# Phase-2 loads kept in program order, and 96-row reads of the normalised activations into alternating partition ranges

## The chip, the cores and the metric

One Trainium2 chip, one core of it. The metric is the device time of one execution in microseconds (us); lower is better. Engines: PE (TensorE matmul, with PEld its weight loads), ACT (ScalarE), DVE (VectorE), POOL (GpSimd), SP (SyncE, which here only issues DMAs). Each engine works through its own queue in order.

## The reference

```
out = depthwise 3x3 convolution of x          # x: 1 x 512 x 512 x 96, bf16
h   = layernorm(out)                          # over the 96 channels
h   = gelu(h @ w1)                            # 96 -> 384
gx  = sqrt(sum over all pixels of h*h + 1e-6) # one number per hidden channel
nx  = gx / (mean of gx + 1e-6)
h   = gamma * (h * nx) + beta + h
out = x + h @ w2                              # 384 -> 96
```

`nx` needs a sum over the whole image, so nothing of the last product can begin before the GELU of every pixel has been squared and summed.

## The kernel before

The image is cut into 128 blocks of 4 rows (2048 pixels), and the kernel runs in two phases.

**Phase 1** goes through the blocks in slots, as a software pipeline. In each slot there are steps of several blocks: load x, transpose it (DVE), convolve (PE), copy out of PSUM (ACT), square (POOL or ACT), statistics (PE), normalise (`stage_norm`, POOL). `stage_write` (SP, four DMAs of 96 KB) stores the normalised block to DRAM as `yn_dram[q]`, 96 channels by 2048 pixels; `stage_read` (SP, one DMA of 384 KB) brings it back into one of six ring tiles `yn_ring` (profile name `ynT`), channels on partitions 0-95. Then comes the MLP step: `w1` times the block (PE), GELU (ACT), the sums of squares (DVE `bn_stats`, or PE products of the result with itself, "gram"). The last 14 blocks use `mlp_tail`: four PE/ACT units per block. Step order for a block b: normalise in slot s, write in s+1, read in s+2, MLP in s+4; in each slot SP gets the reads before the writes. So at the end SP's program order is: read of 125, write of 126, read of 126, write of 127, read of 127, then five loads of x (`xr`) for phase 2 and the first phase-2 load of `ynT`.

**Between the phases** DVE reduces the sums (`second_moments`, `junk` for the gram diagonal, a Newton root), scales `w2` into `W2s`, and phase 2's products can start. Ahead of that, POOL has made the first three `xb` tiles (x plus bias; three buffers).

**Phase 2** makes the output blocks in the order `ORDER` = 123, 125, 127, 118, 1, 2, 0, 4, 5, 120, 6, 8, 3, ... Of 128 blocks, 35 have their GELU output stored in DRAM (`g_dram`, loaded as `gl`, 1536 KB, issued by POOL), 5 are still in SBUF, and 88 are computed again (`recompute`, `cm_unit`: per quarter block three matmuls of 512 columns with `ynT` and `w1p`, and one GELU `gr`). Three of the 88 (123, 125, 127) still have their ring tile; the other 85 read it again (`load_rest`, line 294, SP). That read takes 128 rows, the 96 of the block and 32 of the next one, and rows 96-127 of `w1p` are zero. For position n of `ORDER` the loop at lines 1007-1019 issues the loads of position n+5 (`load_rest`, `load_xr` by POOL), makes `xb` of position n+2 (`stage_xb`, POOL), does 48 small matmuls per block (`stage_mm2`, PE) with four DVE additions into `o_sb`, and stores `o_sb` (`stage_out`, SP). Units of the recomputation are dealt out between the matmuls (`pace`, at least 6 ahead of the even pace).

**What sets the order.** The instructions are placed on each queue by a scheduler that simulates the program and prefers the earlier traced instruction among those ready. Engines wrapped in `InOrder` (`pe, dve, act, pool, sp`) pin each instruction behind the one traced before it on its engine. Phase 1 uses only the wrapped engines. The phase-2 loop uses the wrapped PE, DVE and ACT, but the bare `nc.sync` and `nc.gpsimd` for loads, `xb` and stores, so these may be placed anywhere that their data and buffers allow, ahead of phase-1 instructions too. In the profile wrapped instructions have the line of the wrapper, L35; bare ones keep theirs (L294 `ynT`, L290 `gl`, L279 `xr`, L324 `xb`, L352 stores).

DMAs that SP and ACT issue take eight completion semaphores in turn; a DMA whose semaphore is still in use by the eighth transfer before it carries a wait for that one.

**Setup.** ACT issues the loads of `w1` (three DMAs of 32 rows into `w1_raw`), `w2`, gamma and beta, ahead of its first copy of a convolution. `setup_mlp` (slot 3) subtracts the column mean from `w1` with one DVE instruction and writes `w1p`. `setup_ynt` clears partitions 96-127 of the ring tiles (POOL).

Of the kernel before, what the change touches and what calls it, by code (L numbers as in the profile page):

```python
# [8 lines left out]
ALU = mybir.AluOpType  # L9
# [3 lines left out]
GR = 4  # L13
# [43 lines left out]
def kernel(  # L57
# [10 lines left out]
    nc = tc.nc  # L68
# [53 lines left out]
    def yn_src(q):  # L122
        return yn_dram[q].rearrange("c (r w) -> c r w", r=GR)

    def yn_rows(q):
        return yn_dram[q:q + 2].rearrange("q c (r w) -> (q c) r w", r=GR)[0:128]

    def yn_dst(q, r):
        return yn_dram[q].rearrange("(c i) (r w) -> r c i w", i=NI, r=GR)[r]

# [5 lines left out]
    dwx = consts.tile([9, NI, GR, 32], bf16, name="dwx")  # L136
    eye32 = consts.tile([128, 32], bf16, name="eye32")
    rowsel = consts.tile([128, GR], bf16, name="rowsel")
    w1_raw = consts.tile([C, E], bf16, name="w1_raw")
    w1p = consts.tile([128, E], bf16, name="w1p")  # L140
    Wq = consts.tile([128, NI, 3, GR, 32], bf16, name="Wq")
    w2_sb = consts.tile([128, NCH, C], bf16, name="w2_sb")
    gam_bf = consts.tile([128, NCH], bf16, name="gam_bf")
# [40 lines left out]
    with ExitStack() as p1:  # L184
# [98 lines left out]
        def load_rest(n, sq, pq):  # L283
            q = ORDER[n]
            v = grp.setdefault(q, {})
            if is_held(q):
                v["g"] = gs[q]
            elif is_whole(q):
                v["g"] = late.gl.tile([128, NQ, NCH, QW], bf16, name="gl")
                pq.dma_start(out=v["g"][:].rearrange("p t j w -> p (t j w)"), in_=g_dram[whole.index(q)])  # L290
            else:
                ynt = yn_ring[SLOTS[nth_made[q] % NYT]]
                if q not in KEPT:
                    sq.dma_start(out=ynt[:], in_=yn_rows(q))  # L294
                v["ynt"] = ynt

        def recompute(q, t):
            if t == 0:
                grp[q]["g"] = late.gr.tile([128, NQ, NCH, QW], bf16, name="gr")
            cm_unit(grp[q]["g"], grp[q]["ynt"], t)  # L300

        def cm_unit(g, ynt, t):
            U = banks3()
            for j in range(NCH):
                pe.matmul(quad_out(U[:, j, :]), lhsT=w1p[:, j * 128:(j + 1) * 128],
                          rhs=quad(ynt[:], t), start=True, stop=True)
            act.activation(out=g[:, t, :, :], in_=U, func=ACTF.Gelu_apprx_tanh)

        def px_unit(g, ynt, t):
            Uf = banks3().rearrange("p k w -> p (k w)")  # L310
            for r in range(GR):
                c = r * E
                while c < (r + 1) * E:
                    sz = min((r + 1) * E - c, W - c % W)
                    pe.matmul(Uf[:, c:c + sz], lhsT=ynt[:, r, t * 128:t * 128 + 128],
                              rhs=w1p[:, c - r * E:c - r * E + sz], start=True, stop=True)
                    c += sz
            act.activation(out=g[:, t, :, :].rearrange("p j w -> p (j w)"), in_=Uf, func=ACTF.Gelu_apprx_tanh)
# [66 lines left out]
        for j in range(GR):  # L385
            pool.memset(rowsel[32 * j:32 * j + 32, j:j + 1], 1.0)
        pool.memset(cen[:], 1.0)
        pool.memset(w1p[C:128, :], 0.0)
        dve.memset(SG, 0.0)
        busy(FILL[0])  # L390
        Ud = banks(2)[:, 0, :NI * 9].rearrange("p (i k) -> p i k", i=NI)
# [20 lines left out]
                            pool.tensor_copy(out=o, in_=i_)  # L412

        for i in range(NI):
            act.dma_start(out=w1_raw[i:C:NI, :], in_=w1[chans(i), :])
        act.dma_start(out=w2_sb[:], in_=w2.rearrange("(j p) c -> p j c", p=128))
        with nc.allow_non_contiguous_dma("tiny gamma/beta load"):
            act.dma_start(out=gam_bf[:], in_=grn_gamma.rearrange("(j p) -> p j", p=128))
            act.dma_start(out=bet_bf[:], in_=grn_beta.rearrange("(j p) -> p j", p=128))

        def setup_ynt():
            for t in yn_ring:
                pool.memset(t[C:128, :, :].rearrange("p r w -> p (r w)").bitcast(f32), 0.0)

        def setup_mlp():
            Us = banks(1)[:, 0, :]
            w1m, b2_ps = Us[:, :E], Us[:, E:E + C]
            pe.matmul(w1m, lhsT=cen[:], rhs=w1_raw[:], start=True, stop=True)
            for j in range(NCH):
                pe.matmul(b2_ps, lhsT=bet_bf[:, j:j + 1].to_broadcast([128, 128]), rhs=w2_sb[:, j, :],  # L430
                          start=(j == 0), stop=(j == NCH - 1))
            dve.scalar_tensor_tensor(out=w1p[:C, :], in0=w1m[:C], scalar=-1.0 / C, in1=w1_raw[:],
                                     op0=ALU.mult, op1=ALU.add)
            dve.tensor_copy(out=B2bc_f[:], in_=b2_ps)

        def setup_rest():
# [209 lines left out]

        def stage_read(b):
            t = yn_ring[b % NYT]
            sp.dma_start(out=t[:C], in_=yn_src(b))
            ynts[b] = t  # L650

        bsts = {}
# [19 lines left out]
        def mlp_tail(b, get):  # L672
            if is_held(b) or b < HELD[0]:
                gs[b] = gpool.tile([128, NQ, NCH, QW], bf16, name="g")[:]
            elif b > NBLK - 4:
                gs[b] = late.gr.tile([128, NQ, NCH, QW], bf16, name="gr")[:]
            else:
                gs[b] = g_over
            for t in range(NQ):
                cm = t < cm_quads(b)  # L680
                (cm_unit if cm else px_unit)(gs[b], ynts[b], t)
# [12 lines left out]
            for k in get("moments"):  # L694
                stage_moments(k)
            if cm_quads(b) < NQ:
                grams.extend((b, (NQ - 1) * QC + k * E) for k in range(0, GR, 2))

        def mlp_units(b):
            gs[b] = gpool.tile([128, NQ, NCH, QW], bf16, name="g")[:]  # L700
            g, yt = gs[b], ynts[b]
# [296 lines left out]
    with p2:  # L998
        def out_part(q, o_sb, sub):
            r0 = q * GR  # L1000
            nc.sync.dma_start(
                out=out[0, r0:r0 + GR].rearrange("r w c -> (r w) c").rearrange(
                    "(p g) c -> p g c", g=PXP)[:, sub * GPS:(sub + 1) * GPS],
                in_=o_sb[:, sub * GPS:(sub + 1) * GPS])

        held = None
        for n, q in enumerate(ORDER):
            if n + PRE < NBLK:
                load_rest(n + PRE, nc.sync, nc.gpsimd)
                load_xr(n + PRE, nc.gpsimd)  # L1010
            if 3 <= n + 2 < NBLK:
                stage_xb(ORDER[n + 2], nc.gpsimd, B2c)
            if n == NBLK - 1:
                stage_out(*held)
                held = None
            o_sb = stage_mm2(n, q)
            if held:
                stage_out(*held)
            held = (q, o_sb)
# [30 lines left out]
```

## Time and profile before

| | |
|---|---|
| runs | 1498.53 us median of 3 (1490.1 to 1499.64) |
| the profiled execution | 1500.86 us, span 1499.0 us |
| busy in the span: PE, ACT, POOL, DVE | 93%, 94%, 87%, 79% |
| DMA: bytes, mean rate | 433.08 MB, 289 GB/s |
| phase 1, and the way to the first output block | about 0 to 992 us |
| phase 2 | about 992 to 1499 us |

Times within the profile are us from the start of the span. The views used below: busy time of each engine in stretches of the span; the chain of work that ended last, in order of time (start, length, what; an engine's name followed by q is its queue, the issue of a DMA or a wait in it); the timeline of one engine or queue (start, length, operation, output<-input, and in brackets how long the engine sat idle before it and for what); and the sums of waits. A count "x4" after a row stands for that many instructions in a row.

### The profile page before, as it was taken

The numbers are of one execution on the slowest core, as the hardware profiler recorded it, in microseconds if no ns is written. First come the engines' busy times: TensorE is split into PE (matmuls) and PEld (weight loads), VectorE is DVE, ScalarE is ACT, GpSimd is POOL, SyncE is SP. The second block draws the span as 40 slices with busy tenths as digits, with TensorE's granted clock in tenths as the row PEclk, the third lists the DMA queues.
The fourth block names the chain that finished last, engine by engine and source line by source line (L and its number), as shares of the span: only waits on it lengthen the run. The fifth ranks groups of instructions, "written<-read, shape, count | busy, mean of one in ns | idle before, by whom it ended". The sixth has DMA issues, their size and how long they took to land.

```text
span 1499.0 us, 54229 instructions
## 1 busy us (share of the span) xinstructions
PE 1397.0 (93%) x23125; PEld 813.5 (54%) x23125; DVE 1186.7 (79%) x2135; ACT 1415.5 (94%) x1595; POOL 1300.0 (87%) x922
## 2 busy tenths in 40 slices
PE   7888989999999999999999988689999999999998
PEld 3343444444444444444444445357777777776776
DVE  7748989999999999999999987765555555555555
ACT  6888989999999999999999989789999999999997
POOL 2559899998999999999999997269999999999997
PEclk9999999999999999999999999989999999999999
DMA  5578788888889788888888766569999999999997
GB/s 176 161 205 246 234 250 270 246 258 264 270 248 284 248 273 257 258 244 263 259 258 275 231 212 209 191 220 335 360 361 394 418 419 417 417 407 414 411 411 283
DMA packets 167768, 433.08 MB, mean 289 GB/s; under 512 B 31558, under 2 KB 81318, under 8 KB 163046
## 3 DMA queue, kind: packets, MB, share of 16 engines
q1 hardware_dynamic: 151284, 326.04, 66.1%
q0 software_dynamic: 14880, 103.43, 17.5%
q8 instruction: 181, 2.97, 0.8%
q14 instruction: 61, 0.50, 0.1%
q10 hardware_dynamic: 1362, 0.15, 0.1%
HBM read 273.30 MB, written 156.22 MB: 287 GB/s over the span
## 4 chain that ended last, share of the span: by engine, by line
ACT 22%; POOL 21%; PE 20%; DMA 17%; DVE 10%; issue 5%; SPq 3%; POOLq 0%; ACTq 0%; DVEq 0%
PE PS L35 20%; ACT g L35 16%; POOL xb L324 10%; DMA out_dram<-o_sb 6%; DVE bst L35 6%; ACT y_bf L35 5%; POOL yn L35 4%; SPq L35 3%; POOL ysq L35 3%; DMA yn_dram<-yn 3%; DMA ynT<-yn_dram 3%; DMA rbc<-r_dram 2%; DMA xin<-in_x_dram 2%; DVE xT L35 2%; POOL xr L279 1%
## 5 line engine op out<-in xcount | busy, mean ns | idle before, releaser
L35 ACT ACTIVATE g<-PS 128x512 bf16<-128x512 f32 (+2 forms) x1062 | 728.1, 866 | 20.1 <-PE PS L35 19.5
L35 DVE BATCH_NORM_STATS2 bst<-g 128x6 f32<-128x512 bf16 x1110 | 670.8, 672 | 39.1 <-ACT g L35 38.8
L35 PE MATMUL PS<-ynT,w1p 128*128 128x512 bf16 x2181 | 612.5, 382 | 34.9 <-DMA ynT<-yn_dram 13.0
L35 ACT ACTIVATE gr<-PS 128x1536 bf16<-128x1536 f32 x360 | 498.4, 1450 | 31.9 <-PE PS L35 26.4
L35 POOL TENSOR_TENSOR yn<-y_bf,rbc 128x1536 bf16<-128x1536 bf16 x126 | 391.1, 3106 | 82.2 <-ACT rbc L35 24.6
L35 DVE TENSOR_TENSOR o_sb<-PS,xb 128x384 bf16<-128x384 f32 x512 | 277.4, 556 | 226.6 <-PE PS L35 176.5
L324 POOL TENSOR_TENSOR xb<-xr,B2c 128x1536 f32<-128x1536 bf16 x125 | 390.1, 3132 | 13.5 <-DVE o_sb L35 11.1
L35 PE MATMUL PS<-xT,Wq 64*32 64x511 bf16 (+1 forms) x9198 | 341.2, 390 | 28.0 <-ACT y_bf L35 7.8
L35 POOL TENSOR_TENSOR ysq<-y_bf 128x1536 bf16<-128x1536 bf16 x114 | 313.5, 2750 | 14.9 <-ACT y_bf L35 14.8
L35 PEld LDWEIGHTS <-w1p 128*128 128x128 bf16 x2181 | 171.7, 98 | 233.2 <-issue 127.7
L35 PEld LDWEIGHTS <-gr 128*128 128x128 bf16 x4296 | 213.0, 98 | 69.7 <-issue 13.2
L35 PE MATMUL PS<-W2s,gr 128*128 128x96 bf16 x4224 | 224.2, 206 | 8.2 <-DVE o_sb L35 8.0
L35 PEld LDWEIGHTS <-Wq 64*32 64x32 bf16 x9216 | 112.5, 90 | 195.5 <-issue 147.4
L35 ACT ACTIVATE y_bf<-PS 128x1536 bf16<-128x1536 f32 (+2 forms) x135 | 199.7, 1485 | 17.7 <-PE PS L35 12.8
L35 DVE STREAM_TRANSPOSE xT<-xin 128x576 f32<-128x576 f32 (+1 forms) x256 | 181.5, 748 | 8.3 <-DMA xin<-in_x_dram 8.2
L35 PEld LDWEIGHTS <-g 128*128 128x128 bf16 x1704 | 105.0, 98 | 86.9 <-issue 55.0
L35 PE MATMUL PS<-w1p,ynT 128*128 128x256 bf16 (+2 forms) x822 | 127.0, 276 | 6.3 <-ACT xT L35 3.2
L35 PE MATMUL PS<-g 128*128 128x128 bf16 x1464 | 122.9, 220 | 3.2 <-DVE PS L35 3.0
L35 PEld LDWEIGHTS <-gl 128*128 128x128 bf16 x1680 | 83.0, 98 | 26.5 <-issue 4.9
L35 PE MATMUL PS<-W2s,gl 128*128 128x96 bf16 x1680 | 90.0, 206 | 2.4 <-DVE o_sb L35 2.0
L279 POOL DMA_DIRECT2D xr<-in_x_dram x123 | 68.0, 554 | 16.6 <-POOL xb L324 16.6
L35 PEld LDWEIGHTS <-ynT 128*128 128x128 bf16 x822 | 65.0, 99 | 29.9 <-issue 12.0
(102 smaller groups left out, 554.4 us busy)
## 6 DMA issues: line engine op xcount, KB each, us to landing
xin<-in_x_dram SPq DMA_DIRECT2D x126, 432.0 KB
g_dram<-g SPq DMA_DIRECT2D x105, 512.0 KB
gl<-g_dram POOLq DMA_DIRECT2D x35, 1536.0 KB, 11.0
yn_dram<-yn SPq DMA_DIRECT2D x512, 96.0 KB
ynT<-yn_dram SPq DMA_DIRECT2D x128, 384.0 KB
out_dram<-o_sb SPq DMA_DIRECT2D x127, 384.0 KB
xr<-in_x_dram POOLq DMA_DIRECT2D x123, 384.0 KB, 6.8
ynT<-yn_dram SPq DMA_DIRECT2D x85, 512.0 KB
```

Of the source, the lines that this page charges most:

```text
L35: r = f(*a, **k)
L279: pq.dma_start(out=xr[:], in_=x[0, r0:r0 + GR].rearrange("r w c -> (r w) c").rearrange("(p g) c -> p g c", g=PXP))
L324: pq.tensor_tensor(out=xb[:], in0=grp[q]["xr"][:], in1=bias[:, None, :].to_broadcast([128, PXP, C]), op=ALU.add)
```

## The change

Two things are changed.

The first eight turns of the phase-2 loop issue their loads and make their `xb` on the wrapped `sp` and `pool`, so in program order behind all that was traced before on these two queues; later turns stay as they were. Stores stay on the bare `nc.sync`.

The phase-2 read of a block takes its own 96 rows only (384 KB in place of 512 KB, 85 times). The six ring tiles hold a block on partitions 0-95 (even tiles) or 32-127 (odd tiles), in phase 1 too, and the 32 partitions left over are cleared once. `w1` exists twice, `w1v[0]` with its rows on 0-95 and `w1v[1]` on 32-127, zero elsewhere, and each use takes the copy of its tile. So there are three more DMAs from `w1` on ACT's queue, one more small POOL memset, and the column mean is subtracted by six DVE instructions of 32 partitions in place of one of 96.

```diff
-    def yn_rows(q):
-        return yn_dram[q:q + 2].rearrange("q c (r w) -> (q c) r w", r=GR)[0:128]
+    def rows_of(slot):
+        return slice(32, 128) if slot % 2 else slice(0, C)
+    def rest_of(slot):
+        return slice(0, 32) if slot % 2 else slice(C, 128)
+    w1v = [consts.tile([128, E], bf16, name=f"w1_{i}") for i in range(2)]
+    w1_raw = w1v[0]
...
# load_rest
-                ynt = yn_ring[SLOTS[nth_made[q] % NYT]]
+                slot = SLOTS[nth_made[q] % NYT]
+                ynt = yn_ring[slot]
                 if q not in KEPT:
-                    sq.dma_start(out=ynt[:], in_=yn_rows(q))
-                v["ynt"] = ynt
+                    sq.dma_start(out=ynt[rows_of(slot)], in_=yn_src(q))
+                v["ynt"], v["w1"] = ynt, w1v[slot % 2]
...
# setup
         for i in range(NI):
-            act.dma_start(out=w1_raw[i:C:NI, :], in_=w1[chans(i), :])
+            act.dma_start(out=w1v[0][i:C:NI, :], in_=w1[chans(i), :])
+        for i in range(NI):
+            act.dma_start(out=w1v[1][32 + i:128:NI, :], in_=w1[chans(i), :])
...
# setup_mlp
-            dve.scalar_tensor_tensor(out=w1p[:C, :], in0=w1m[:C], scalar=-1.0 / C, in1=w1_raw[:],
-                                     op0=ALU.mult, op1=ALU.add)
+            for i in range(2):
+                for p in range(32 * i, 32 * i + C, 32):
+                    k = slice(p, p + 32)
+                    dve.scalar_tensor_tensor(out=w1v[i][k, :], in0=w1m[k], scalar=-1.0 / C, in1=w1v[i][k, :],
+                                             op0=ALU.mult, op1=ALU.add)
...
# stage_read
-            sp.dma_start(out=t[:C], in_=yn_src(b))
+            sp.dma_start(out=t[rows_of(b % NYT)], in_=yn_src(b))
...
# the phase-2 loop
+        FIRST = 8
         for n, q in enumerate(ORDER):
+            sq, pq = (sp, pool) if n < FIRST else (nc.sync, nc.gpsimd)
             if n + PRE < NBLK:
-                load_rest(n + PRE, nc.sync, nc.gpsimd)
-                load_xr(n + PRE, nc.gpsimd)
+                load_rest(n + PRE, sq, pq)
+                load_xr(n + PRE, pq)
             if 3 <= n + 2 < NBLK:
-                stage_xb(ORDER[n + 2], nc.gpsimd, B2c)
+                stage_xb(ORDER[n + 2], pq, B2c)
```

More of the change, by code (lines that the diff above doesn't have):

```diff
@@ L138 @@
     rowsel = consts.tile([128, GR], bf16, name="rowsel")
-    w1_raw = consts.tile([C, E], bf16, name="w1_raw")
-    w1p = consts.tile([128, E], bf16, name="w1p")
+    def rows_of(slot):
[4 more added lines that the diff above has]
+    w1_raw = w1v[0]
     Wq = consts.tile([128, NI, 3, GR, 32], bf16, name="Wq")
@@ L299, in recompute, with cm_unit @@
                 grp[q]["g"] = late.gr.tile([128, NQ, NCH, QW], bf16, name="gr")
-            cm_unit(grp[q]["g"], grp[q]["ynt"], t)
-        def cm_unit(g, ynt, t):
+            cm_unit(grp[q]["g"], grp[q]["ynt"], grp[q]["w1"], t)
+        def cm_unit(g, ynt, w1p, t):
             U = banks3()
@@ L307, in cm_unit, with px_unit @@
             act.activation(out=g[:, t, :, :], in_=U, func=ACTF.Gelu_apprx_tanh)
[L309 removed]
+        def px_unit(g, ynt, w1p, t):
             Uf = banks3().rearrange("p k w -> p (k w)")
@@ L387 @@
         pool.memset(cen[:], 1.0)
-        pool.memset(w1p[C:128, :], 0.0)
+        for i in range(2):
+            pool.memset(w1v[i][rest_of(i), :], 0.0)
         dve.memset(SG, 0.0)
@@ L421, in setup_ynt @@
         def setup_ynt():
-            for t in yn_ring:
-                pool.memset(t[C:128, :, :].rearrange("p r w -> p (r w)").bitcast(f32), 0.0)
+            for i, t in enumerate(yn_ring):
+                pool.memset(t[rest_of(i), :, :].rearrange("p r w -> p (r w)").bitcast(f32), 0.0)
         def setup_mlp():
@@ L427, in setup_mlp @@
             w1m, b2_ps = Us[:, :E], Us[:, E:E + C]
-            pe.matmul(w1m, lhsT=cen[:], rhs=w1_raw[:], start=True, stop=True)
+            pe.matmul(w1m, lhsT=cen[:], rhs=w1_raw[:C, :], start=True, stop=True)
             for j in range(NCH):
@@ L431, in setup_mlp @@
                           start=(j == 0), stop=(j == NCH - 1))
-            dve.scalar_tensor_tensor(out=w1p[:C, :], in0=w1m[:C], scalar=-1.0 / C, in1=w1_raw[:],
-                                     op0=ALU.mult, op1=ALU.add)
+            for i in range(2):
+                for p in range(32 * i, 32 * i + C, 32):
+                    k = slice(p, p + 32)
+                    dve.scalar_tensor_tensor(out=w1v[i][k, :], in0=w1m[k], scalar=-1.0 / C, in1=w1v[i][k, :],
+                                             op0=ALU.mult, op1=ALU.add)
             dve.tensor_copy(out=B2bc_f[:], in_=b2_ps)
@@ L680, in mlp_tail @@
                 cm = t < cm_quads(b)
-                (cm_unit if cm else px_unit)(gs[b], ynts[b], t)
+                (cm_unit if cm else px_unit)(gs[b], ynts[b], w1v[b % NYT % 2], t)
                 gram_next(1)
@@ L700, in mlp_units @@
             gs[b] = gpool.tile([128, NQ, NCH, QW], bf16, name="g")[:]
-            g, yt = gs[b], ynts[b]
+            g, yt, w1p = gs[b], ynts[b], w1v[b % NYT % 2]
             px0 = QC * (cm_quads(b) - 2)
```

## The prediction

> **What bounds the kernel now.** I began with the busy time of each engine in stretches of the span, to see which stage has air in it.
>
> ```profile
> 750.00:900.00 150.00, 139.51 (x2503) 70.29 (x2488) 141.81 (x244) 145.71 (x204) 139.76 (x104) 1.00 0.78 243
> 900.00:1000.00 100.00, 74.50 (x630) 46.45 (x629) 74.09 (x145) 84.49 (x63) 48.44 (x32) 0.90 0.62 202
> 1040.00:1080.00 40.00, 40.00 (x589) 29.74 (x587) 22.72 (x42) 39.68 (x30) 37.77 (x22) 1.00 0.96 350
> 1300.00:1400.00 100.00, 95.92 (x1391) 70.44 (x1391) 53.25 (x99) 93.46 (x68) 97.04 (x58) 1.00 1.02 410
> ```
>
> Columns: stretch, length, then PE, PEld, DVE, ACT, POOL busy, granted clock, DMA share, GB/s. Phase 1 is bound by ACT (145.71 of 150). Phase 2 is tight everywhere: at first PE is full, later POOL leads with 97.04 of 100 and the DMA engines are full. Only 900 to 1000, the change of phase, has room. There I read the chain that ended last:
>
> ```profile
> 952.56 0.82 PE PS L35 x3
> 953.39 0.35 SPq L294
> 953.91 6.00 DMA ynT<-yn_dram
> 959.96 3.39 PE PS L35 x15
> ...
> 970.25 0.82 PE PS L35 x3
> 971.09 0.34 SPq L294
> 971.60 4.75 DMA ynT<-yn_dram
> 976.40 1.47 PE PS L35 x3
> ```
>
> PE ends the last matmuls of block 124, which frees a ring tile; only then can a phase-2 load (L294, position 5 of the order) go out; behind it in SP's queue stands the read of block 125, for which PE waits. The same comes again at 971: 126, then the load of position 7, then the read of 127. SP's queue shows that the read was otherwise ready, since the writes of block 125 had been issued by 942.64:
>
> ```profile
> 940.16 2.48 SPq L35 DMA_DIRECT2D yn_dram<-yn  x4
> 953.39 0.35 SPq L294 DMA_DIRECT2D ynT<-yn_dram  x1
> 953.91 1.09 SPq L35 DMA_DIRECT2D ynT<-yn_dram  x1
> 955.05 3.34 SPq L35 DMA_DIRECT2D yn_dram<-yn  x4
> ```
>
> **Step 1, the two loads leave the head of SP's queue.** ACT sets the pace here, so I price the stalls on it:
>
> ```profile
> 949.44 5.75 ACT L35 ACTIVATE g<-PS 128x1536 bf16<-128x1536 f32 x4
> 961.52 1.45 ACT L35 ACTIVATE gr<-PS 128x1536 bf16<-128x1536 f32 x1 [6.33 <-PE PS L35]
> 963.38 4.13 ACT L35 ACTIVATE gr<-PS 128x1536 bf16<-128x1536 f32 x3 [0.41 <-PE PS L35]
> 967.39 5.50 ACT L35 ACTIVATE g<-PS 128x1536 bf16<-128x1536 f32 x4
> 977.90 1.45 ACT L35 ACTIVATE gr<-PS 128x1536 bf16<-128x1536 f32 x1 [5.01 <-PE PS L35]
> 979.82 4.13 ACT L35 ACTIVATE gr<-PS 128x1536 bf16<-128x1536 f32 x3 [0.47 <-PE PS L35]
> ```
>
> Four GELUs start 5.39 apart when nothing is missing (944.05 to 949.44), so 1.347 each. The next was due at 954.83 and began at 961.52: 6.69. Its successor came after 1.86 in place of 1.347: 0.51. Then 972.78 was due and 977.90 came: 5.12, and again 0.57. Sum **12.9 us**.
>
> What is late next? In earlier slots the read goes out 1.7 us after the end of the writes (932.60 to 934.29, 938.11 to 939.81), and a read takes at most the 6.0 above. Read of 125: 944.4, landed by 950.4, wanted by PE at 953.4. POOL ends the normalising of 125, 126, 127 at 938.7, 941.7 and 944.8, so the writes of 126 follow at 944.8 to 947.3, their read at 949.0 to 955.0, wanted at 958.8; writes of 127 to 951.9, read 953.6 to 959.6, wanted at 964.2. Slacks of 3.0, 3.8 and 4.6 us: both stalls go whole, -12.9. If reads took 4 us longer, about 1 us of it would stay.
>
> **Step 2, the sums behind them.** The five `xr` loads stand behind the read of 127 on SP and move from 972.0 to about 954.0, and POOL's first three `xb` from 977.4-986.6 to about 959.4-968.6. Two tiny DVE products of 128x3 at 981.78 and 983.62 took 1.80 and 3.04 us while those `xb` ran; larger ones (128x36) at 976, before them, took 0.2 us. The gram that DVE needs next ended on PE at 984.85, but `junk` began at 987.21, 2.4 us late. Now DVE gets there (968.9) as the `xb` end. I take -1.0, ends 0 and -2.4.
>
> **Step 3, what the moved instructions are now queued behind.** On SP each pinned load stands behind the store traced before it: position 7 behind the store of turn 0 (998.3 now, about 984.5 then), 8 behind that of turn 1, 10 and 11 behind turns 3 and 4 (about 995.7 and 1001). The units that need them come about 999, 1004, 1011 and 1016 (6 units ahead, 0.69 unit per quarter of a 3.8 us block). With 6 us to land, each has 8 us to spare: 0. On POOL the two `gl` loads (now hoisted to 945.07) go behind the third `xb` (about 970) and the eighth turn (about 1004); they land in 11.0 us (median) and are wanted about 1002 and 1024: 0, and 4 to 6 us if POOL or the DMAs run 10 us behind. `xr` of position n+5 now follows `xb` of n+1, not its own source `xb` of n. In the row of 998 to 1042 each `xr` directly behind its `xb` starts 0.30 late ("0.30 <-POOL xb"); some five such waits go. I count -1.5, ends 0 and -2, as POOL sets the end later on.
>
> **Step 4, smaller loads.** 85 loads lose 128 KB each. Between 1100 and 1460 there are 62 of them: 8.1 MB of 147.12, 5.6% of a DMA time that is full. What waits for what there:
>
> ```profile
> DVE o_sb L35 <- DMA out_dram<-o_sb: 26.4, 21, 3.0
> POOL xr L279 <- POOL xb L324: 10.7, 36, 0.3
> PE PS L35 <- DVE o_sb L35: 9.6, 18, 1.9
> POOL xb L324 <- DVE o_sb L35: 0.6, 1, 0.6
> ```
>
> Stores delay DVE, and DVE delays PE by 9.6; but POOL, with 286.9 (`xb`) + 49.7 (`xr`) + 14.4 (`gl`) of 360 busy and 10.7 waiting on itself, waits for DVE 0.6 in all. POOL hides the gain: 0. If POOL were not the cover, PE's 9.6 bounds it, so the ends are 0 and -8. No row shows a load into partitions 32-127; the nearest is the 384 KB read above (6.00 and 4.75), and 8 us of slack covers either.
>
> [...]
>
> **Step 5, setup.** ACT's queue issues `w1` in steps of 0.64 (5.59, 6.23, 6.87), gamma at 8.15 and beta at 12.35; only then comes the first copy, 12.78, after 4.88 idle, though its convolution ended near 11.2. Beta's semaphore was that of the x load of block 4, whose transpose also starts on landing, 12.36. Three more transfers cost 3 x 0.64 = 1.9 if nothing hides them, and the semaphores shift: a later `w1` piece would wait for 12.35 and `w2`, gamma and beta follow with 0.6 each. The copy would come near 14.6: +1.8. Ends: -1.4 (no wait hit, issue ends about 10.9, the copy at 11.4) and +2.7 (beta waits for a later x load). The DVE subtraction takes 0.47 until the next begins; six take 2.8, +2.35. Its successors reach PE's spread at 33.10, PE comes there at 34.84: 1.74 hides, +0.6 is left, ends 0 and +2.4. POOL's extra memset (0.42) ends before its wait of 2.74 for DVE at 5.50: 0. Cleared partitions and matmuls keep count and size: 0.
>
> **Sum:** -12.9 - 1.0 - 1.5 + 0 + 1.8 + 0.6 = **-13.0**. Against its own execution, 1500.86, that is 1487.9; that one lies 2.3 above the median of the runs, so for the runs I say 1498.53 - 13.0 = **1485.5**. With the ends of steps 2, 3 and 5 this case reaches from 1479 to 1491.
>
> **Rivals.** (A) The smaller loads pay as well: full DMAs and 26.4 us of store waits speak for it, POOL's 0.6 against it. -8 more: 1477.5, chance 0.19. (B) The gain is eaten in POOL's queue. The scheduler places turns from 8 on anew; now 34 of 123 `xr` stand not directly behind their `xb`. A turn with the wait takes 4.02 (998.39 to 1002.39), one in a pair 3.64 (1022.97 to 1030.25, halved). If all became direct, 34 x 0.38 = 13: 1498.5. Against it: the rule of placing is unchanged. That the change does not do what it says, because a bare load still floats ahead, gives 1498.53 + 2.4 = 1501; against it, later loads need tiles or buffers that phase 2 frees. Together 0.18. (C) Slower: the four pinned loads behind the stores (positions 7, 8, 10, 11) land too late for their units. With DMAs full a store took 12.1 us to land; from 8 + 6 = 14 us on, each us costs one per load. At 21 us that is 4 x 7 = 28: 1513.5. Against it: the DMA share there is 0.88. Chance 0.08.
>
> **Chances.** Forecast 0.55. The measurement tells about 1% from no change, below 1483.5 here. A third of the forecast's range lies below it (0.19), with A 0.38; the rest of it and B are within 1%, 0.54; C is 0.08. The range leaves out C and the far ends of A and B: 1475 to 1498.
>
> **What would show it.** Right: no L294 load before the end of phase 1; the reads of 125 to 127 out by about 954; no PE wait for `ynT` there; first `o_sb` about 14 us less the setup's cost earlier; the first ACT copy at about 14.6; from 1100 on store waits shrink while POOL stays 97% busy. Wrong: new PE waits for `ynT` after 990 (C), more 0.30 waits on POOL (B), or a shorter phase 2 (A).

## The result, and the profile after

The changed kernel is **slower**: 1513.76 us, the median of 4 runs (1510.76 to 1514.91), against 1497.53 for the kernel before, timed beside it. The ratio is **1.0114, 95% interval [1.0075, 1.0153]**, so some 17 us are lost where 13 were forecast as a gain; the range that was given ended at 1498.0. The profiled execution took 1514.82 us, its span 1513.0.

The loss is not where the change of phase is. That part went almost as predicted. `W2s`, the last thing that phase 2 waits for, was ready at 991.4 before and at 980.9 after. From there to the end took 507.6 us before and 532.1 after. So phase 2 lost 24.5 us, and what lies ahead of it gained 10.5.

Busy time by stretch, after (columns as in the prediction: stretch, length, PE, PEld, DVE, ACT, POOL, granted clock, DMA share, GB/s):

```profile
900.00:1000.00 100.00, 81.99 (x833) 53.50 (x831) 78.84 (x162) 96.36 (x73) 61.45 (x37) 1.00 0.64 196
1040.00:1080.00 40.00, 40.00 (x591) 29.85 (x590) 22.64 (x43) 39.39 (x29) 37.62 (x22) 1.00 1.01 356
1300.00:1400.00 100.00, 90.20 (x1311) 66.52 (x1311) 50.90 (x95) 88.46 (x64) 90.02 (x54) 1.00 1.02 371
```

From 900 to 1000 ACT went from 84.49 to 96.36 busy: the holes at the change of phase are closed. From 1300 to 1400 every engine does less: PE 95.92 to 90.20, with 1311 matmuls in place of 1391, and POOL 97.04 to 90.02. No engine became the bound. Only the DMA share still reads 1.02, as before, and with it the rate fell from 410 to 371 GB/s. The engines that move the data are as busy as they were and move less.

What ends last in phase 2: the chain of work that ended last, 1100 to 1420, its shares by line, of the kernel before:

```profile
by line: PE PS L35 41.1%; DMA out_dram<-o_sb 24.9%; POOL xb L324 24.5%; DVE o_sb L35 4.1%; issue 2.6%; POOL xr L279 2.3%; POOL gl L290 0.9%; DVEq L35 0.1%; POOLq L324 0.0%; POOLq L290 0.0%; POOLq L279 0.0%
```

The same view of the kernel after:

```profile
by line: PE PS L35 50.0%; DMA out_dram<-o_sb 40.1%; POOL xb L329 6.8%; DVE o_sb L35 3.4%; issue 1.2%; POOL xr L283 0.8%; POOL gl L294 0.3%; DVEq L35 0.1%; POOLq L329 0.0%; POOLq L283 0.0%
```

POOL's `xb` nearly leaves the chain (24.5% to 6.8%), and landing stores take its place (24.9% to 40.1%). The chain of before has six single stores, of 12.1 to 15.2 us; that of after has eight, of 14.4 to 20.0. Three of them (start, length, what):

```profile
1202.12 15.25 DMA out_dram<-o_sb
...
1231.95 19.98 DMA out_dram<-o_sb
...
1289.14 16.45 DMA out_dram<-o_sb
```

The sums of waits from 1120 to 1460, after (what waits for what: us in all, times, longest):

```profile
DVE o_sb L35 <- DMA out_dram<-o_sb: 51.5, 28, 4.0
...
PE PS L35 <- DVE o_sb L35: 29.2, 19, 3.4
POOL xb L329 <- DVE o_sb L35: 21.2, 14, 4.5
```

The prediction read 26.4, 9.6 and 0.6 in the same rows of before. I read this as one ripple. A store lands late, so its `o_sb` buffer is not free and DVE's additions wait; PE waits for DVE's release of PSUM, and POOL for DVE's release of an `xb` buffer. POOL's queue, which had hidden the store waits, now waits for them too.

### The profile page after: what moved, and what is told of

Same layout as the page of the kernel before. It is cut to its first block, busy times and chain, and to the rows that moved or that the text cites. A ratio compares the mean times of both kernels' runs of the same rounds, so it can differ in the third digit from the quotient of the medians.

```text
span 1513.0 us, 54235 instructions
## 1 busy us (share of the span) xinstructions
PE 1395.9 (92%) x23125; PEld 812.6 (54%) x23125; DVE 1185.3 (78%) x2140; ACT 1416.0 (94%) x1595; POOL 1301.4 (86%) x923
## 4 chain that ended last, share of the span: by engine, by line
PE 23%; DMA 14%; ACT 11%; POOL 4%; DVE 2%; issue 2%; SPq 1%; POOLq 0%; DVEq 0%; ACTq 0%
PE PS L35 23%; DMA out_dram<-o_sb 10%; ACT g L35 7%; ACT y_bf L35 2%; POOL xb L329 1%; SPq L35 1%; POOL ysq L35 1%; DVE o_sb L35 1%; POOL yn L35 1%; DMA yn_dram<-yn 1%; ACT xT L35 1%; ACT gr L35 1%; DMA rbc<-r_dram 1%; DVE bst L35 1%; DMA ynT<-yn_dram 1%
## 5 line engine op out<-in xcount | busy, mean ns | idle before, releaser
L35 PE MATMUL PS<-ynT,w 128*128 128x512 bf16 x2181 | 611.3, 382 | 23.5 <-ACT g L35 5.4
L35 POOL TENSOR_TENSOR yn<-y_bf,rbc 128x1536 bf16<-128x1536 bf16 x126 | 391.3, 3108 | 85.4 <-ACT rbc L35 26.4
L329 POOL TENSOR_TENSOR xb<-xr,B2c 128x1536 f32<-128x1536 bf16 x118 | 368.7, 3131 | 26.6 <-DVE o_sb L35 24.1
L35 PEld LDWEIGHTS <-w 128*128 128x128 bf16 x2181 | 171.8, 98 | 222.0 <-issue 127.2
L35 PE MATMUL PS<-W2s,gr 128*128 128x96 bf16 x4224 | 225.2, 207 | 26.4 <-DVE o_sb L35 26.1
L35 PE MATMUL PS<-w,ynT 128*128 128x256 bf16 (+2 forms) x822 | 125.4, 273 | 7.8 <-ACT xT L35 3.2
L283 POOL DMA_DIRECT2D xr<-in_x_dram x115 | 63.7, 555 | 14.2 <-POOL xb L329 14.2
## 6 DMA issues: line engine op xcount, KB each, us to landing
gl<-g_dram POOLq DMA_DIRECT2D x35, 1536.0 KB, 12.1
```

Of the source, the lines that this page charges most:

```text
L35: r = f(*a, **k)
L283: pq.dma_start(out=xr[:], in_=x[0, r0:r0 + GR].rearrange("r w c -> (r w) c").rearrange("(p g) c -> p g c", g=PXP))
L329: pq.tensor_tensor(out=xb[:], in0=grp[q]["xr"][:], in1=bias[:, None, :].to_broadcast([128, PXP, C]), op=ALU.add)
```

## The experiments

Two theories stood against each other from the start: either the 96-row reads themselves make the DMA engines slower, or the new order on the queues (pinned loads behind stores, `xr` and `gl` in other places) does. The setup was a third suspect. The ratios below are all to the kernel before, timed on the same chip. To compare two experiments I take the difference of their ratios times 1497.5 us. The profile of each kernel is one execution, so differences of one or two microseconds between two profiles show little. In the code cuts `...` stands for lines left out.

### The order alone

The kernel before with the pinned first eight turns; loads of 128 rows, one `w1`, old setup. `load_xr` and `stage_xb` get `pq` in the same way.

```diff
+        FIRST = 8
         for n, q in enumerate(ORDER):
+            sq, pq = (sp, pool) if n < FIRST else (nc.sync, nc.gpsimd)
...
-                load_rest(n + PRE, nc.sync, nc.gpsimd)
+                load_rest(n + PRE, sq, pq)
...
```

> The kernel before with the program order of the first eight phase-2 turns alone; loads of 128 rows, one w1. Its queues hold the same instructions in the same order as the changed kernel's from phase 2 on. Theory (the 96-row shape of the loads costs the DMA engines more than the 128-row one, and that is the whole loss): the two stalls go, phase 2 stays about 500 us from the fourth xb to the end, 1497.5 - 13 = 1484 us, DMA rate 1100 to 1460 near 409 GB/s. Rival A (the order of the later turns, newly placed, lengthens phase 2): as slow as the changed kernel, 1510 to 1515 us. Rival B (the range 32-127 is at fault, not the count of rows): also 1484 us; it parts from the theory in e3.

1486.16 us, ratio **0.9897 [0.9860, 0.9933]**: -15.4 us. `W2s` comes at 973.2 and phase 2 takes 506.8 us, the same as before. So the half of the change that the prediction priced in its steps 1 to 3 was worth what it said in sum, and phase 2 doesn't mind the order.

### The rows alone

The changed kernel with nothing pinned.

```diff
-        FIRST = 8
+        FIRST = 0
```

> The changed kernel with the first eight turns left to the scheduler as before; 96-row loads in alternating ranges, two copies of w1. Its queues have the order of the kernel before. Theory and rival B: the stalls are back and the slow loads stay, 1513.8 + 12 = 1526 us. Rival A: 1497.5 + 3 for the setup = 1500 us.

1527.42 us, ratio **1.0185 [1.0134, 1.0236]**: +27.7 us. `W2s` comes at 1004.0, and phase 2 takes 528.4. The loss is there without any pinned load, so none of the pinned loads behind stores is its cause.

### 96 rows in phase 2 only, always on partitions 0-95

The order alone, plus only the smaller phase-2 read; old setup, one `w1`, no alternation.

```diff
-                    sq.dma_start(out=ynt[:], in_=yn_rows(q))
+                    sq.dma_start(out=ynt[:C], in_=yn_src(q))
```

> As e1, but the 85 phase-2 loads take 96 rows, always into partitions 0-95; one w1, setup as before. Theory: the 96-row shape costs wherever it lands, so phase 2 is at least as slow as in the changed kernel; with 3 us less setup 1508 to 1515 us, more if the alternation had helped. Rival B: 96 rows into 0-95 are harmless and 25% fewer bytes, 1478 to 1484 us. Rival A: 1510 to 1515 us.

1507.25 us, ratio **1.0061 [1.0032, 1.0089]**. Against the order alone this one line costs 0.0164, or **24.6 us**, and phase 2 takes 533.1 in place of 506.8. The stretch 1100 to 1420, with the order alone (columns as above):

```profile
1100.00:1420.00 320.00, 310.10 (x4506) 228.90 (x4504) 173.04 (x320) 305.97 (x222) 309.70 (x189) 1.00 1.02 411
```

And with the 96-row loads:

```profile
1100.00:1420.00 320.00, 301.10 (x4325) 221.41 (x4323) 167.06 (x309) 293.11 (x212) 295.09 (x181) 0.99 1.02 370
```

The rate falls from 411 to 370 GB/s, a tenth, at the same DMA share. A read that is a quarter smaller saves 5 to 6% of the bytes that phase 2 moves for an output block; the engines lose 10% of their rate. The balance is about 5% of 507 us, which is the loss.

### The same bytes over all 128 partitions

The order alone, and each phase-2 read brings its 384 KB as 128 rows of 3072 bytes. The pixels then don't lie where the product wants them, so the recomputed blocks are other numbers; every instruction is the same.

```diff
-                    sq.dma_start(out=ynt[:], in_=yn_rows(q))
+                    sq.dma_start(out=ynt[:].rearrange("p r w -> p (r w)")[:, :C * GR * W // 128],
+                                 in_=yn_dram[q].rearrange("c s -> (c s)").rearrange("(p w) -> p w", p=128))
```

> As e1, but each of the 85 phase-2 loads brings exactly the 393216 bytes that the 96-row load brings, spread over 128 partitions of 3072 bytes. The block's rows lie in the wrong places then, so what is recomputed from them is not the reference's; the work of all engines is the same. Theory: the bytes are no trouble, the 96-row shape is; 1476 to 1484 us, DMA share of 1100 to 1460 under 1.00. If instead the loads' own source or their size were at fault: 1508 to 1515 us.

1480.1 us, ratio **0.9869 [0.9810, 0.9929]**, phase 2 502.3 us. The bytes are those of the run before this, and it is 28.8 us faster. What hurts is therefore the shape, 96 partitions, and not the transfer's size. The DMA share, which I expected under 1.00, reads 1.01 from 1100 to 1420, at 392 GB/s. Against the order alone the 4 us are inside both intervals, so a gain from fewer bytes is not shown in the time. In the sums of waits of this kernel it is (1100 to 1420):

```profile
DVE o_sb L35 <- DMA out_dram<-o_sb: 1.0, 1, 1.0
```

It was 19.9 with the order alone. The stores stop mattering, and POOL takes over: its `xb` is 55.6% of the chain there. This is the cover of step 4: with cheaper reads POOL hides most of what is saved.

### Shapes of the load by themselves, first try

Only transfers: 36 loads of one shape back to back on SP, then 30 turns of one load, one store and, on POOL's queue, one `xr` load; the same for every shape.

> Nothing of the kernel but loads from x in the shapes in question, six stages one after the other: 128 rows of 4096 bytes; 96 rows into partitions 0-95; 96 rows into 0-95 and 32-127 in turn; 128 rows of 3072 bytes; 96 rows as three loads of 32 rows on every fourth partition; 96 rows as loads of 64 and 32 rows. Each stage has 36 loads into a ring of six tiles, then 30 turns of one such load, one store of 384 KB and one load of 384 KB by POOL. The output is left unwritten but for the stores. Theory (the 96-row shape makes the DMA engines get in each other's way): a 96-row load takes at least as long as a 128-row one, 1.3 us each or more in a row, and in the turns with store and POOL load the 96-row stages take no less time per turn than the 128-row stage although they move 10% fewer bytes; 128 rows of 3072 bytes take three quarters, 1.0 us, and the turns shrink by a tenth. Whether every fourth partition is as quick as 128 rows tells if the spread over partitions decides or the count of rows per engine. Rival (a 96-row load is quicker when it stands alone, and only its mixing with the phase-2 traffic hurts): 1.0 us in a row.

Inconclusive for what it was made for. Nothing tied POOL's queue to the stages, so its 180 loads ran ahead beside the first stages, the last issued at 299.8 us; 128 and 96 rows met different traffic. Later stages were clean: SP's issues for 37 blocks took 51.4 us with 96 rows in turn on 0-95 and 32-127, 72.9 with three loads of 32 rows on every fourth partition for a block, and 55.5 with loads of 64 and 32 rows. So cutting a block into several loads doesn't help.

### POOL pinned for the whole of phase 2

The order alone, with POOL's queue in program order in all turns. Then no `xr` stands directly behind the `xb` it needs. The expectation below counts 81 such loads with the order alone; its trace has 48 that wait 0.30 us each, 14.2 us in all.

```diff
-            sq, pq = (sp, pool) if n < FIRST else (nc.sync, nc.gpsimd)
+            sq, pq = sp if n < FIRST else nc.sync, pool
```

> As e1, but POOL's loads and xb of all phase-2 turns stay in program order, so that no xr load stands directly behind the xb that frees its tile: 81 waits of 0.30 us on POOL go. If POOL's queue alone bounds phase 2 from 1100 on: up to 20 us off e1, 1466 us. If the DMA engines, full at 1.02, bind as much: 0 to 6 us off, 1480 to 1486 us, with POOL waiting for DVE in place of its own xb.

1485.24 us, ratio **0.9884 [0.9848, 0.9921]**: no different from the order alone. POOL's busy time from 1100 to 1420 falls from 309.7 to 302.7 us, and the rate stays at 411 GB/s. Some 14 us of small waits on an engine that is busy for 97% of the time were worth nothing that can be measured. In their place POOL waits for DVE, which it had not done in this stretch with the order alone (sums of waits, 1100 to 1420):

```profile
DVE o_sb L35 <- DMA out_dram<-o_sb: 24.7, 15, 4.0
POOL xb L35 <- DVE o_sb L35: 13.2, 17, 4.9
```

DVE's own wait for stores was 19.9 there. So what POOL saved went into waiting for stores that land late.

### The whole setup, without alternation

The changed kernel with both copies of `w1` set up, but every block on partitions 0-95, in phase 1 too, and the first copy always used.

```diff
-                    sq.dma_start(out=ynt[rows_of(slot)], in_=yn_src(q))
-                v["ynt"], v["w1"] = ynt, w1v[slot % 2]
+                    sq.dma_start(out=ynt[:C], in_=yn_src(q))
+                v["ynt"], v["w1"] = ynt, w1v[0]
...
```

> The changed kernel without the alternation: both copies of w1 are set up, all blocks lie on partitions 0-95 in both phases, and only the first copy is used. Against e3 (1507.3, same loads, old setup) it prices the setup: 3 to 4 us, 1511 us. Against the changed kernel (1513.8) it prices the alternation: if alternation helps, this one is slower than 1514; if it does nothing, 1511 to 1514.

1515.84 us, ratio **1.0111 [1.0071, 1.0151]**. The changed kernel has 1.0114, so the alternation brings nothing that can be measured (the median lies above the 1514 that the expectation named, but so does its kernel before, 1499.68 against 1497.53). Against 96 rows without the new setup (1.0061) the setup costs 0.0050, or 7.5 us; the intervals overlap, so the trace has to show it, which is done two experiments on.

### Shapes by themselves, second try

As the first, with POOL's loads tied to their stage: POOL reads a mark from each ring tile before its next load.

> Loads from x alone, as in m1, but POOL's loads are tied to the stage they belong to. First five stages of 36 loads each: 128 rows of 4096 bytes; 96 rows into partitions 0-95; into 32-127; in turn; 128 rows of 3072 bytes. Then the same five shapes in 30 turns of one such load, one store of 384 KB by SP and one load of 384 KB by POOL. The output is left unwritten but for the stores. Theory: alone, 128 rows take 1.26 us (416 GB/s), 128 short rows about 1.0, and 96 rows 1.40 as in m1's stage of alternating ranges, whichever range, so 280 GB/s; in the turns 96 rows cost no less than 128. Rival (the ranges differ): 0-95 and 32-127 lie apart by more than a tenth, or alternation beats both.

The timeline of SP's queue, each line one stage of 36 loads (start, length, operation, count; "low" is 96 rows on 0-95, "high" 32-127, "turns" both in turn, "short" 128 rows of 3072 bytes):

```profile
0.75 43.56 SPq L33 DMA_DIRECT2D whole<-in_x_dram  x36
44.35 59.71 SPq L33 DMA_DIRECT2D low<-in_x_dram  x36
104.10 54.68 SPq L33 DMA_DIRECT2D high<-in_x_dram  x36
158.82 53.23 SPq L33 DMA_DIRECT2D turns<-in_x_dram  x36
212.09 38.14 SPq L33 DMA_DIRECT2D short<-in_x_dram  x36
```

Without the first ten loads of each stage, which fill the queue, that is 1.28 us per load of 128 rows (512 KB, 410 GB/s), **1.70** for 96 rows on 0-95 (384 KB, 231 GB/s), 1.50 on 32-127, 1.48 in turn, and 0.98 for the same 384 KB over 128 partitions. I had expected 1.40 for 96 rows in either range. A 96-row load alone takes *longer* than the 128-row load that it replaces, and, as the rival of this run had it, the two ranges differ, by 13%. The page of this run shows the same in 40 slices of the span, DMA busy in tenths and the rate:

```profile
DMA  9999999999999999999999999999999999999996
GB/s 352 410 378 228 232 233 256 263 263 265 267 267 361 402 414 420 417 416 417 390 383 387 391 373 370 380 380 392 397 382 379 370 376 390 376 414 418 418 414 270
```

The DMA share is 9 in all slices but the last, at 410 as at 230 GB/s. The packets of these loads (one row each) took 163 ns on average with 128 rows, 291 with 96 on 0-95, 257 on 32-127, 253 in turn and 125 with 3072 bytes; in each stage their sum, divided by 16, is 1.02 to 1.03 of the time. So with 96 rows the 16 engines are on average as busy as with 128, and each row takes longer. In the mixed turns, though, the sign was the other one: some 3.2 us per turn with 128 rows, 3.1 with 96. That left open why the kernel lost.

### The three extra transfers alone, and the six subtractions alone

Two runs that each add one part of the setup to the order alone, with the extra copy never used.

```diff
...
+        for i in range(NI):
+            act.dma_start(out=w1_two[32 + i:128:NI, :], in_=w1[chans(i), :])
```

> As e1, with the three more loads of w1 on ACT's queue (into a tile that nothing reads), and none of the added DVE work. The setup cost 7 us from e3 to e7 where 2.4 were predicted. If the ACT queue's wait is the larger share: 4 to 6 us over e1, 1490 to 1492 us; by the prediction's step 1.8 us over, 1488.

```diff
-            dve.scalar_tensor_tensor(out=w1p[:C, :], in0=w1m[:C], scalar=-1.0 / C, in1=w1_raw[:], ...)
+            for w in (w1p, w1_two):
+                for p in range(0, C, 32):
+                    k = slice(p, p + 32)
+                    dve.scalar_tensor_tensor(out=w[k, :], in0=w1m[k], scalar=-1.0 / C, in1=w1_raw[k, :], ...)
```

> As e1, with the column mean subtracted by six DVE instructions of 32 partitions (the second three into a tile that nothing reads), and no added loads. If DVE's share is the larger: 4 to 6 us over e1, 1490 to 1492 us; by the prediction's step 0.6 us over, 1487.

1489.2 us, ratio 0.9932 [0.9909, 0.9955], and 1492.19 us, ratio 0.9945 [0.9916, 0.9975]. Both lie above the order alone (0.9897), by 5 and 7 us, but with overlapping intervals; their sum of 12 stands against the 7.5 us of the whole setup above, so the time alone doesn't settle the sizes. The trace is sharper. ACT's third copy of `rbc` is a point that all kernels pass. ACT's timeline with the order alone:

```profile
32.73 1.02 ACT L35 ACTIVATE rbc<-PS 128x1024 bf16<-128x1024 f32 x1 [0.90 <-PE PS L35]
```

With the three transfers:

```profile
35.90 1.02 ACT L35 ACTIVATE rbc<-PS 128x1024 bf16<-128x1024 f32 x1 [0.89 <-PE PS L35]
```

With the six subtractions:

```profile
36.09 1.02 ACT L35 ACTIVATE rbc<-PS 128x1024 bf16<-128x1024 f32 x1 [4.26 <-PE PS L35]
```

With both, in the run without alternation:

```profile
39.35 1.02 ACT L35 ACTIVATE rbc<-PS 128x1024 bf16<-128x1024 f32 x1 [4.28 <-PE PS L35]
```

The transfers cost 3.2 us there, the subtractions 3.4, both together 6.6. At this point they add up.

### The order on SP alone

SP's loads pinned, POOL's left as before.

```diff
-            sq, pq = (sp, pool) if n < FIRST else (nc.sync, nc.gpsimd)
+            sq, pq = sp if n < FIRST else nc.sync, nc.gpsimd
```

> As e1, but only SP's loads of the first eight turns are pinned; POOL's loads and xb are placed as in the kernel before. Theory (the gain is the two loads that leave the head of SP's queue): as e1, 1484 to 1488 us. If the order on POOL (large loads issued before the phase ends, xr behind its own xb) had a share: 1.5 us or more above e1.

1491.34 us, ratio **0.9953 [0.9928, 0.9979]**, 5 us above the order alone by the medians and 8 by the ratios, and above the 1484 to 1488 of the theory; the intervals just overlap. So SP's order by itself is worth 7 us, and POOL's order seems to have a share. POOL's timeline of this kernel has the two `gl` loads early again, 3 MB at 938.66:

```profile
938.66 1.29 POOL L290 DMA_DIRECT2D gl<-g_dram  x2 [0.31 <-POOL yn L35]
```

On SP's queue a block's read then waits longer for its writes. The queue of this kernel:

```profile
939.45 2.72 SPq L35 DMA_DIRECT2D yn_dram<-yn  x4
952.42 0.31 SPq L35 DMA_DIRECT2D ynT<-yn_dram  x1
```

The queue with the order alone:

```profile
940.25 2.49 SPq L35 DMA_DIRECT2D yn_dram<-yn  x4
946.36 0.31 SPq L35 DMA_DIRECT2D ynT<-yn_dram  x1
```

13.0 us from writes to read, against 6.1. From the end of the fourth issue to the read it is 10.3 us here and 3.6 with the order alone. The `gl` loads, issued just ahead of these writes, took 11.0 us each to land in the kernel before (median). That they hold the writes up is my reading of this.

`W2s` comes 6.0 us later (979.2 against 973.2), but little of that is the late read itself. ACT is 1.8 us behind already at 918, before these loads go out, and then loses about 1 us to a late block. The larger part comes by way of `xr`: these loads stand behind the late reads on SP, and POOL's first three `xb`, which begin 4.2 to 4.5 us after the first of them in this kernel, the order alone and the changed kernel, move from 955.96 to 962.01. There they run beside two DVE products of 128x36 that took 0.2 us each in the kernel before; with the order alone one of them took 2.16. POOL's and DVE's timelines of this kernel:

```profile
962.01 9.27 POOL L35 TENSOR_TENSOR xb<-xr,B2bc_f 128x1536 f32<-128x1536 bf16 x3 [22.05 <-PE PS L35]
965.58 2.67 DVE L35 TENSOR_TENSOR parts<-mv 128x36 f32<-128x36 f32 x1
968.29 3.04 DVE L35 TENSOR_TENSOR parts<-parts,mv 128x36 f32<-128x36 f32 x1
```

So `junk` begins 6.1 us after its gram, where it was 2.7 with the order alone: 3.4 us of the 6.0. What I put down to the `gl` loads is therefore some 4 us in this pair of profiles; the 5 to 8 us of the time are not shown to be all theirs.

### The kernel's traffic without the kernel

The mixed turns again, with what they had lacked: in three turns of ten a `gl` load of 1536 KB in rows of 12288 bytes.

> Only transfers, no matmul and no output block: the kernel's phase-2 traffic per turn, one load of normalised activations in a given shape and one 384 KB store on SP's queue, one 384 KB xr load on POOL's queue, and in three turns of ten a 1536 KB gl load of 12288-byte rows, which the turns of m2_shapes lacked. Four stages of 48 turns: 128 rows, 96 rows on 0-95, 96 rows in turn on 0-95 and 32-127, 128 rows of 3072 bytes. In m2_shapes a turn took 3.19 us with 128 rows and 3.09 with 96 on 0-95, 10% fewer bytes and 3% less time. A turn is now 1.69 MB or 1.56 MB. Theory 1: the 96-row load hurts the kernel because its packets slow those of the other queues, the long ones of gl above all; then 96 rows take longer than 128 here, about 4.3 us a turn against 4.15, 365 GB/s against 410, as the kernel's phase 2 does. Theory 2: with other queues in the mix the lost rate stays a property of the load's own share; then a 96-row turn is still some 0.1 us shorter than a 128-row one, 380 to 390 GB/s, and the kernel's loss needs its waits (stores that land late, buffers) on top. Both expect 128 rows of 3072 bytes to be shortest, about 3.8 us.

Busy time in stretches within the four stages (128 rows; 96 on 0-95; 96 in turn; 128 of 3072 bytes). The columns here are stretch, length, POOL busy, clock, DMA share, GB/s:

```profile
40.00:190.00 150.00, 31.23 (x82) 1.00 1.02 421
240.00:400.00 160.00, 32.16 (x85) 1.00 1.02 379
455.00:610.00 155.00, 29.80 (x79) 1.00 1.02 375
670.00:800.00 130.00, 29.41 (x78) 1.00 1.02 419
```

The rate falls from 421 to 379 and 375 GB/s, a tenth, as in the kernel. Taken between SP's issues of the loads of turns 10 and 40, a turn takes 4.28 us with 128 rows, 4.36 and 4.42 with 96, and 3.94 with the 96 rows' bytes over 128 partitions. With the long rows in the mix, the smaller load makes the turn longer. By how much depends on the turns that are taken: other stretches of 30 or 40 turns give 0.03 to 0.17 us for 96 rows on 0-95 and 0.12 to 0.17 in turn. Times 85 that would be 2 to 14 us of the 24.6. Where the rest comes from is not measured. The kernel has 0.7 such loads per output block and not one, so it saves 6% of its bytes and not 7%, for the same tenth of the rate; and its stores are waited for.

The single packets agree. From the trace's DMA packet records, mean duration in ns:

| packet, queue | this run: 128 rows | 96 on 0-95 | 96 in turn | kernel before | kernel after |
|---|---|---|---|---|---|
| `ynT` load, 4096 B, SP | 159 | 180 | 186 | 162 | 192 |
| `xr` load, 6144 B, POOL | 236 | 273 | 279 | 243 | 281 |
| `gl` load, 12288 B, POOL | 461 | 512 | 509 | 477 | 523 |
| 3072 B, SP | 121 | 129 | 129 | 122 | 129 |

(Kernel: 1100 to 1420.) The packets of *both* queues get longer, those of POOL's loads too, though those loads are the same as before. With 3072-byte rows over 128 partitions they stay at 121, 237 and 460 in this run. In the kernel with such rows the means are 123, 255 and 503, so the means of POOL's packets grow there too, without a loss of time; but the medians are those of before (121, 234 and 460), and with 96 rows the medians of POOL's packets rise as well (246 and 491 in the kernel after).

## Why the prediction was wrong

**Step 1** held. No load of L294 stands ahead of the last reads, PE waits for no `ynT` there, and ACT runs through (ACT's timeline after, four instructions to a line):

```profile
952.95 5.75 ACT L35 ACTIVATE g<-PS 128x1536 bf16<-128x1536 f32 x4
958.31 5.76 ACT L35 ACTIVATE gr<-PS 128x1536 bf16<-128x1536 f32 x4
963.65 5.79 ACT L35 ACTIVATE g<-PS 128x1536 bf16<-128x1536 f32 x4
969.00 5.82 ACT L35 ACTIVATE gr<-PS 128x1536 bf16<-128x1536 f32 x4
```

The four groups start 5.3 to 5.4 us apart, with no idle time in front. The last read went out at 958.3 and not at 953.6, but the whole end of phase 1 was as much later (the last copy `y_bf` began at 892.6, 887.8 before). From that copy to the end of the gram the way shrank by 13.9 us, where the step said 12.9 (by 15.6 with the order alone). **Step 2** came out above its size: the two small products took 0.17 us each, clear of POOL's `xb`, and `junk` began 0.7 us after its gram in place of 2.4, so 1.6 and not 1.0 was gained. From the last copy `y_bf` to `W2s` the way shrank from 103.6 to 88.3 us: 15.3, where the two steps said 13.9. In time the order alone gave -15.4, by its interval -10 to -21. That this is the very sum of steps 1 to 3 is luck: in its profile `junk` still began 2.7 us late, so step 2 gained nothing there, and step 3's term was worth nothing, as follows.

**Step 3** had the right sum for the order as built, but one reason and one omission were wrong. The 0.30 us waits of `xr` are worth nothing, as the run with POOL pinned throughout shows. And the two `gl` loads, priced at 0 because they would land in time for their own readers, by my reading delay SP's writes and reads while they run (13.0 us from writes to read, against 6.1), and through them the `xb` and the small products of step 2: some 4 us in the trace of the kernel that has them early. I had asked who waits for these loads, not what they delay while they run. The pinned loads on SP cost nothing that shows, as said: phase 2 takes 506.8 us with them and 507.6 before.

**Step 4 is where it failed**, with +24.6 us where the sum had 0. It priced the smaller load by its bytes, with ends of 0 and -8, on the ground that "85 loads lose 128 KB each" and the DMA time is full. A full DMA share says at most that time on the DMA engines is scarce, and bytes are its price only as long as the rate stays; here it fell from 411 to 370 GB/s at a share of 1.02. I bounded the gain from both sides and the loss not at all, though I had noted that no row shows a load into partitions 32-127. The nearest row that I named, the phase-1 read of 96 rows (6.00 and 4.75 us to land), sits in a stage with a DMA share of 0.62; a latency there says nothing of a rate where the engines are full. What was measured: by itself a load of 96 rows on 0-95 takes 1.70 us, one of 128 rows 1.28. With the two ranges in turn it is 1.48, and in the kernel the alternation brought nothing that can be measured (ratio 1.0114 with it, 1.0111 without).

Why do 96 rows cost more? The simplest reading would be that fewer engines carry the load. Against it speaks that the mean share of the 16 is as full as with 128 rows (1.02 to 1.03) while each row takes longer, 291 ns alone against 163. In the kernel the packets of POOL's queue grow longer too (`xr` from 243 to 281 ns), though its loads are the same. But no run here shows which engine wrote which partition, and this stays open.

**Step 5** was mis-sized: +2.4, measured 6.6 us in the trace by 39 us, and 7.5 in time. The first copy came near where it was put (13.85; 14.6 said), but that was against one execution. Six other profiles with the old transfers have this copy at 11.77 to 12.26, where before's own has 12.78. In the run with the transfers alone it came at 14.13, 2.2 us after the order alone (11.95), and lost 1.0 more in PE's work ahead of the first `rbc`. The six subtractions were priced at +0.6, because PE was taken to reach its spread 1.74 us after they would be done. Those 1.74 were PE's wait for a read of `ynT` in that one execution (PE's timeline of the kernel before):

```profile
32.06 1.44 PE L35 MATMUL PS<-ynT,w1p 128*128 128x512 bf16 x3 [1.74 <-DMA ynT<-yn_dram]
```

With the order alone, whose setup is the same, there is no such wait, and the third `rbc` comes at 32.73 and not at 35.66. Against that one execution the changed kernel's 38.00 looks like the predicted 2.4. Now DVE is what PE waits for (PE's timeline after):

```profile
36.93 1.03 PE L35 MATMUL PS<-ident_b,rstdx 128*128 128x128 bf16 x8 [3.72 <-DVE rstdx L35]
```

The six take 3.40 us, where 2.8 was put, in place of 0.47, and all of it shows: with the subtractions alone the third `rbc` is 3.4 us later.

**The rivals.** A fell: the smaller loads don't pay, they cost. B fell: 48 `xr` loads wait 0.30 us for their own `xb`, where 56 did before, so there were fewer of these waits and not more. Its price was also miscounted: 89 of the 123 loads stand directly behind some `xb` in the kernel before, but only those 56 behind the one that they need. C gave the time, 1513.5, by a mechanism that isn't there: no PE wait for `ynT` appears, and the loss is present without any pinned load. That the DMA engines themselves become slower was in none of them. Two slips of the prediction change nothing: 8.1 of 147.12 MB is 5.5% and not 5.6, and 998.39 to 1002.39 is 4.00 us and not 4.02.

**The sum**, as measured: -15.4 (order), +24.6 (96 rows), +7.5 (setup), +0.4 (alternation) = **+17.1 us**, a ratio of 1.0114. The terms are steps along one row of kernels (before, order alone, 96 rows, whole setup, changed kernel), so they add up to the total by construction, and each carries an interval of several microseconds. The order alone is the version to keep: 1486.16 us, 0.9897 [0.9860, 0.9933]; pinning POOL throughout adds nothing to it.

## What to carry to other kernels

Where the DMA share is full (1.02 here), price a transfer by the time that its shape takes on the DMA engines, and not by its bytes: here a 96-partition read with 25% fewer bytes took longer alone than the 128-partition one (1.70 us against 1.28), and in the kernel the packets of POOL's unchanged loads grew by 10 to 16%. Read GB/s beside the DMA share, since the share alone reads full in both cases (1.02 at 411 and at 370 GB/s), and when no row shows the new shape, leave an end of the range on the loss side. Moving phase-2 loads out of the way of the chain at the change of phase was worth 1% by itself, and cover that is a wait in a single execution (the 1.74 us here) shouldn't be booked as cover.

## What was not expected of the hardware

- The DMA share stays at its top (1.02 to 1.03 by the packets) while the rate of SP's loads alone falls from 410 to 231 GB/s (96 rows on partitions 0-95) or 263 (32-127). The share reads 1.01 with 3072-byte rows too, where stores are hardly waited for (1.0 us): it doesn't tell whether the transfers hold the kernel up. The place in SBUF matters as well: 1.70 us per load on 0-95 against 1.50 on 32-127.
- With a load of another shape on SP's queue, the packets of POOL's queue get longer: `xr` from 243 to 281 ns, `gl` from 477 to 523.
- Three loads of 32 rows on every fourth partition take 2.0 us for one block, longer than one load of 96 rows (1.5 to 1.7) or of 128 (1.3).
- DVE products of 128x3 that took 1.80 and 3.04 us while POOL ran its `xb` took 0.17 clear of them, and products of 128x36 that took 0.2 before took 2.67 and 3.04 beside the `xb` in the kernel with only SP's order pinned.
